# One product for the last 64 tokens of seven batches, and loads that wait for the transposed q

## The chip, the cores and the metric

The kernel runs on one core of a Trainium2 chip. The metric is the device time of one execution in microseconds (us). The kernel before takes 296.39 us, the median of three runs from 295.75 to 305.15.

## The reference

Inputs are q, k and v of shape (batch 8, heads 8, 576 tokens, 64 features) and two weight matrices. The first half is a linear attention whose feature map is a ReLU weighted by the cosine and the sine of the token's position; the second half is a feed-forward network with a sigmoid-approximated gelu.

```python
q_p = phi(q, cos_w, sin_w)          # max(x,0)*cos, max(x,0)*sin: 128 features
k_p = phi(k, cos_w, sin_w)
kv = einsum('bhsf,bhsd->bhfd', k_p, v);  z = sum(k_p over s)
num = einsum('bhsf,bhfd->bhsd', q_p, kv)
den = einsum('bhsf,bhf->bhs', q_p, z) + 1e-6
x = (num / den) as (8*576 tokens, 512)
h = x @ w_in                        # 512 -> 2048
out = (h * sigmoid(1.702*h)) @ w_out   # 2048 -> 512
```

## The kernel before

The work goes batch by batch, and the kernel calls the work of one batch a block. Instructions run on each engine in the order in which the program lists them; the order is written out by hand, and only the waits between engines are added by the framework.

A block b has two stages on TensorE. In the first, `mm1` multiplies w_in by the transposed x of the batch: for each of 16 groups of 128 hidden features (fc) four matmuls of 512 columns, that is 512 of the 576 tokens, followed by a gelu on ScalarE. The other 64 tokens of the batch, its tail, go through `mm1_tail`, where each of 64 matmuls loads a 128x128 block of w_in and streams 64 columns (L284). In the second stage `mm2` multiplies by w_out, 16 matmuls of 512 columns for each group of 128 tokens. Groups t = 0 to 3 are the 512 tokens of the batch. Group t = 4 is made of two tails, that of an even batch and that of the odd one after it; it is computed in the odd blocks, ahead of t = 0. Each group is copied out of PSUM by ScalarE (L309) to one of four ysb buffers and stored by a DMA on POOL's queue (L312).

Beside the matmuls of block b, the attention of batch b+1 is prepared. Early in the block VectorE computes the features of q (`trig_q`, L154), and SyncE issues five DMA transposes that write qT (`qturn_dma`, L184), the fifth with the 64 tail tokens. Once q's buffer has been read, POOL issues the load of q for batch b+2 (`load_q`, L112 and L114); then VectorE computes the features of k (L141) and copies v (L162), and POOL issues the loads of k and v (`load`, L109). With fc = 15 TensorE computes kv (L202). During the second stage it computes the numerator and denominator of five token groups (`num_mm`, L215), VectorE divides (`num_div`, L223 to L227), and SyncE issues a DMA transpose of each result into the x of the next block (`xturn_dma`, L253), four pieces of 128 tokens and one of 64. Numbers 0 to 3 come between halves of t = 0 and t = 1, number 4 in t = 2.

POOL's queue is one list: loads and stores are issued in the order of the program, and a store that is not ready holds the loads after it. DMAs issued by POOL run on queue q0, those issued by SyncE, the transposes among them, on q1; both use the same 16 DMA engines.

Blocks 0 and 1 differ: batch 0 is loaded in a different layout, the pipeline is filled, the weights are loaded in between, and block 1's first five feature groups are computed in four pieces of columns. In block 0 POOL already waits once for the transposed q (L415) before it loads the inputs of batch 2.

Of the kernel before, what the change touches and what calls it, by code (L numbers as in the profile page):

```python
# [9 lines left out]
F32 = mybir.dt.float32  # L10
BF16 = mybir.dt.bfloat16
AF = mybir.ActivationFunctionType
# [7 lines left out]
def kernel(  # L20
# [9 lines left out]
    nc = tc.nc  # L30
    B, H, S, D = q.shape
    d_model = H * D
    d_ff = moe_w_in.shape[1]
    KC = d_model // 128
    FC = d_ff // 128
    NS = S // 64
    MT = 512
# [3 lines left out]
    one = ctx.enter_context(tc.tile_pool(name="one", bufs=1))  # L41
    xpool = ctx.enter_context(tc.tile_pool(name="xpool", bufs=2))
    gpool = ctx.enter_context(tc.tile_pool(name="gpool", bufs=20))
    ypool = ctx.enter_context(tc.tile_pool(name="ypool", bufs=4))
    small = ctx.enter_context(tc.tile_pool(name="small", bufs=3))
    pmm = ctx.enter_context(tc.tile_pool(name="pmm", bufs=4, space=PSUM))
# [51 lines left out]
    qT = one.tile([128, H, 640], BF16, name="qT")  # L98
    w_in_sb = one.tile([128, KC, d_ff], BF16, name="w_in_sb")
    w_out_sb = one.tile([128, FC, d_model], BF16, name="w_out_sb")  # L100
# [7 lines left out]
    def load(t, src, b):  # L108
        nc.gpsimd.dma_start(out=t, in_=src_of(src, b))  # L109

    def load_q(b):
        nc.gpsimd.dma_start(out=qf[:, 0:2048].rearrange("p (h e) -> p h e", h=H),  # L112
                            in_=q[b, :, 0:512, :].rearrange("h (p c) d -> p h (c d)", c=4))
        nc.gpsimd.dma_start(out=qf[0:64, 2048:2560].rearrange("p (h e) -> p h e", h=H),  # L114
                            in_=q[b, :, 512:S, :].rearrange("h p d -> p h d"))
# [7 lines left out]
    gate = const.tile([1, 4], F32)  # L123
# [10 lines left out]
    def trig(dst, src, j, act=False):  # L134
        i = src[:, :, ts(j, 64)]
        for cs, w in enumerate((cosw, sinw)):
            o = dst[:, j, :, ts(cs, 64)]
            if act:
                nc.scalar.activation(o, i, AF.Relu, scale=w[:, j:j + 1])
            else:  # L140
                nc.vector.tensor_scalar(o, i, 0.0, w[:, j:j + 1], op0=MAX, op1=MUL)  # L141

    def trig_q(c, act=False):
        n = 128 if c < 4 else 64
        if c < 4:
            i = qf[:, 0:2048].rearrange("p (h c d) -> p c h d", h=H, c=4)[:, c]
        else:
            i = qf[0:64, 2048:2560].rearrange("p (h d) -> p h d", h=H)
        for cs, w in enumerate((cosw, sinw)):
            o, sc = qn[0:n, c, :, ts(cs, 64)], w[0:n, NS + c:NS + c + 1]  # L150
            if act:
                nc.scalar.activation(o, i, AF.Relu, scale=sc)
            else:
                nc.vector.tensor_scalar(o, i, 0.0, sc, op0=MAX, op1=MUL)  # L154

    def vcopy(i0, i1, act=False):
        o = vt[:, :, i0:i1, 0:64].rearrange("p j i e -> p i j e")
        i = vf[:, i0:i1].rearrange("p i (j e) -> p i j e", e=64)
        if act:
            nc.scalar.activation(o, i, AF.Copy)  # L160
        else:
            nc.vector.tensor_copy(o, i)  # L162
# [19 lines left out]
    def qturn_dma(c):  # L182
        n = 128 if c < 4 else 64
        nc.sync.dma_start_transpose(out=qT[:, :, c * 128:c * 128 + n],  # L184
                                    in_=qn[0:n, c].rearrange("p h f -> p (h f)"))
# [3 lines left out]
    def kv_open(i0=0, i1=NI):  # L189
        t = pat.tile([128, 2, 512], F32, name="at")  # L190
        for i in range(i0, i1):
            st["kv", i] = t[:, :, ds((i - i0) * 65, 65)]
        st["ps", i0] = t[:, :, 0:(i1 - i0) * 65]
        if i0 == 0:
            st["kvs"] = small.tile([128, 2, NI, VW], BF16, name="kvs", bufs=2)
# [9 lines left out]
    def kv_evac(i0, i1):  # L205
        o = st["kvs"][:, :, i0:i1, 0:65]
        nc.vector.tensor_copy(o, st["ps", i0].rearrange("p hh (i e) -> p hh i e", e=65))  # L207
# [23 lines left out]
    x = {}  # L231

    def x_open(b):
        x[b] = xpool.tile([128, KC, S], BF16, name="xT")

    def xturn_mm(c):
        ps, xn = nums[c]
# [5 lines left out]
    def xturn_evac(b, c):  # L243
        ps = nums.pop(c)[0]
        n = 128 if c < 4 else 64
        i = ps[:, :, 264:392].bitcast(BF16).rearrange("p a (k t) -> p a k t", k=2)[:, :, :, 0:n]
        o = x[b][:, :, c * 128:c * 128 + n].rearrange("p (a k) t -> p a k t", a=2)
        nc.scalar.activation(o, i, AF.Copy)

    def xturn_dma(b, c):  # L250
        xn = nums.pop(c)[1]
        n = 128 if c < 4 else 64
        nc.sync.dma_start_transpose(out=x[b][:, :, c * 128:c * 128 + n],  # L253
                                    in_=xn[0:n].rearrange("p a h e -> p (a h e)"))


    gT = {}
# [14 lines left out]
    def mm1(b, fc):  # L272
        mm1_part(b, fc, 0, MT)
        gelu(fc)

    gt = {}

    def mm1_tail(b, half):
        if half == 0 and b % 2 == 0:
            gt[0] = gpool.tile([128, FC, 128], BF16, name="gtail", bufs=2)  # L280
        hps = pmm.tile([128, 8, 64], F32, name="mm")
        for f in range(8):
            for kc in range(KC):
                nc.tensor.matmul(hps[:, f], w_in_sb[:, kc, ts(half * 8 + f, 128)], x[b][:, kc, MT:S],  # L284
                                 start=(kc == 0), stop=(kc == KC - 1))
        nc.scalar.activation(gt[0][:, ts(half, 8), ts(b % 2, 64)], hps, AF.Gelu_apprx_sigmoid)  # L286

    yp = {}
    out_j = out[0:S].rearrange("(p j) d -> j p d", j=NS)

    def rows(b, t):

        if t == 4:
            return [(64 * u, 64, out_j[NS - 1] if b + u == 1 else out[(b + u) * S - 64:(b + u) * S])
                    for u in range(2)]
        if b == 0:
            return [(64 * u, 64, out_j[2 * t + u]) for u in range(2)]
        return [(0, 128, out[b * S:b * S + 512].rearrange("(p c) d -> c p d", c=4)[t])]

    def mm2(b, t, lo, hi, c0=0, c1=d_model, last=False):  # L300
        if lo == 0:
            yp[t, c0] = pmm.tile([128, d_model], F32, name="mm")
        for fc in range(lo, hi):
            w = gT[fc][:, ts(t, 128)] if t < 4 else gt[0][:, fc, :]
            nc.tensor.matmul(yp[t, c0][:, c0:c1], w, w_out_sb[:, fc, c0:c1],  # L305
                             start=(fc == 0), stop=(fc == FC - 1))
        if hi == FC:
            ysb = ypool.tile([128, d_model], F32, name="ysb")
            nc.scalar.activation(ysb[:, c0:c1], yp[t, c0][:, c0:c1], AF.Identity)  # L309
            for p0, n, dst in rows(b, t):  # L310
                eng = nc.sync if last else nc.gpsimd
                eng.dma_start(out=dst[:, c0:c1], in_=ysb[p0:p0 + n, c0:c1])  # L312
# [78 lines left out]
    qturn_pe(4)  # L391
    qevac(4)
    x_open(0)
    start_block(0)

# [9 lines left out]
        trig(kr, kf, j)  # L405
    for fc in range(5, FC):
        mm1(0, fc)
    mm1_tail(0, 0)
    mm1_tail(0, 1)
    for c in range(5):  # L410
        trig_q(c, act=(c > 2))
        qturn_dma(c)
# [34 lines left out]
    for b in range(1, B):  # L447
        nb = b + 1 if b + 1 < B else None
        f0 = 5 if b == 1 else 0
        for fc in range(f0, FC):  # L450
            if nb is not None and fc == f0:
                for c in range(5):
                    trig_q(c)
                    qturn_dma(c)
                if nb + 1 < B:
                    load_q(nb + 1)
            if nb is not None and fc == f0 + 1:
                for j in range(NS):
                    trig(kr, kf, j)
                vcopy(0, 4)  # L460
                if nb + 1 < B:
                    load(kf, k, nb + 1)
                    load(vf, v, nb + 1)
            if nb is not None and fc == 15:
                kv_open()
                kv_mm(0, 4, vt_rhs, 0, 65)
                kv_evac(0, 4)
            mm1(b, fc)
        mm1_tail(b, 0)
        mm1_tail(b, 1)  # L470
        if nb is not None:
            x_open(nb)
        if b % 2:
            mm2(b, 4, 0, FC)
        for t in range(4):
            last = nb is None and t == 3
            if last:
                mm2(b, t, 0, FC, 0, 256)
                mm2(b, t, 0, FC, 256, 512, last=True)
                continue  # L480
            mm2(b, t, 0, 8)
            if nb is not None and t < 3:
                num_mm(2 * t)
                num_div(2 * t)
                xturn_dma(nb, 2 * t)
            mm2(b, t, 8, 16)
            if nb is not None and t < 2:
                num_mm(2 * t + 1)
                num_div(2 * t + 1)
                xturn_dma(nb, 2 * t + 1)  # L490
# [30 lines left out]
```

## Time and profile before

| | us |
|---|---|
| median of the runs | 296.39 |
| profiled execution, its own time | 295.57 |
| its span, first to last instruction | 293.9 |
| TensorE busy (share of the span) | 283.1 (96%) |
| first product, 512 columns and pieces (L264) | 113.6 |
| second product of the 512 tokens (L305) | 116.0 |
| first product of the tails (L284) | 16.2 |
| second product of the tails (L305 from gtail) | 13.6 |
| numerator (L215) and kv (L202, from vt) | 15.9 and 8.8 |
| VectorE busy, ScalarE busy | 123.8, 128.0 |
| DMA queue q0 / q1, share of 16 engines | 43.3% / 28.4% |

Busy time counts an instruction from its start to its modelled end, and overlapping matmuls are counted once. Below, a chain in order of time lists what TensorE did without such overlap: start, duration, engine and line, and how many instructions were merged. Of a DMA the profile gives the issue on the queue of the engine that starts it, and the time from issue to landing.

In block 1 the first product starts at 52.3 us, kv runs at 66.95, the tail at 69.11, t = 4 at 71.03, the first numerator at 76.15 and the next block at 89.45. Block 2 lasts from 89.45 to 121.45, block 3 from there to 156.91.

### The profile page before, as it was taken

Reading aid. Unit: us, or ns where it says so; the run is one execution under the profiler, and the core shown is the slowest. Engines: PE = TensorE matmul, PEld = TensorE weight load, DVE = VectorE, ACT = ScalarE, POOL = GpSimd, SP = SyncE. Lnnn points to the kernel's source line nnn. Section 1 sums busy time; section 2 is a strip of 40 time slices with the busy share of each in tenths; the row PEclk is TensorE's granted clock in tenths of the full one; section 3 lists DMA queues with packets and bytes.
Section 4 is the critical chain, followed back from the end, with each engine's and each line's share of the span. In section 5 each row is a group of like instructions: output and inputs, shape, how many; then the busy total and the mean of one; then the engine's idle time right before and its main releaser. Section 6 shows DMA issues by size and latency. Waiting matters only on the chain.

```text
span 293.9 us, 6796 instructions
## 1 busy us (share of the span) xinstructions
PE 283.1 (96%) x2832; PEld 155.7 (53%) x2871; DVE 123.8 (42%) x355; ACT 128.0 (44%) x220; POOL 81.9 (28%) x96
## 2 busy tenths in 40 slices
PE   8879999999999999999999999999999999999993
PEld 4775546746544465446454465446454465445443
DVE  4674513791369125930269115950159304200000
ACT  7847642674115721465114641265114651166121
POOL 6361002635216501470215601290114300100111
PEclk9999999999999999999999999999999999999999
DMA  7999997999999876779249983889258402400112
GB/s 254 239 219 276 351 180 109 326 312 228 323 272 184 240 294 142 156 192 365 71 128 171 221 333 96 151 193 386 85 140 153 93 2 75 115 36 0 38 71 73
DMA packets 64238, 53.59 MB, mean 182 GB/s; under 512 B 49552, under 2 KB 56336, under 8 KB 64208
## 3 DMA queue, kind: packets, MB, share of 16 engines
q0 software_dynamic: 13792, 38.87, 43.3%
q1 hardware_dynamic: 50416, 14.30, 28.4%
q8 instruction: 22, 0.36, 0.5%
q14 instruction: 8, 0.07, 0.1%
HBM read 36.70 MB, written 9.44 MB: 157 GB/s over the span
## 4 chain that ended last, share of the span: by engine, by line
PE 95%; issue 1%; DVE 1%; ACT 1%; ACTq 0%
PE mm L305 42%; PE mm L264 37%; PE mm L284 5%; PE at L202 4%; PE at L215 3%; PE mm L317 3%; PE at L241 1%; DVE xn L227 1%; PE mm L170 1%; ACT g L269 1%; DVE inv L225 0%; DVE den L223 0%; ACT ysb L309 0%; DVE warm L76 0%; ACTq L269 0%
## 5 line engine op out<-in xcount | busy, mean ns | idle before, releaser
L305 PE MATMUL mm<-w_out_sb,g 128*128 128x512 bf16 (+1 forms) x509 | 116.0, 372 | 1.1 <-issue 0.2
L264 PE MATMUL mm<-xT,w_in_sb 128*128 128x512 bf16 (+1 forms) x593 | 113.6, 345 | 0.8
L312 POOL DMA_DIRECT2D out_dram<-ysb x44 | 50.7, 1152 | 169.7 <-ACT ysb L309 162.9
L269 ACT ACTIVATE g<-mm 128x512 bf16<-128x512 f32 x128 | 75.6, 598 | 39.6 <-PE mm L264 39.6
L264 PEld LDWEIGHTS <-w_in_sb 128*128 128x128 bf16 x608 | 53.8, 98 | 55.2
L305 PEld LDWEIGHTS <-g 128*128 128x128 bf16 x528 | 49.0, 98 | 50.2
L309 ACT ACTIVATE ysb<-mm 128x512 f32<-128x512 f32 (+1 forms) x37 | 21.7, 586 | 108.1 <-PE mm L305 101.9
L223 DVE TENSOR_SCALAR den<-at 128x8 f32<-128x8 f32 x40 | 6.6, 166 | 60.6 <-PE at L215 60.6
L227 DVE TENSOR_TENSOR xn<-at,inv 128x512 bf16<-128x512 f32 x40 | 27.7, 691 | 2.4 <-DMA xT<-xn 1.0
L207 DVE CAST kvs<-at 128x520 bf16<-128x520 f32 (+1 forms) x9 | 5.8, 642 | 51.3 <-PE at L202 51.2
L141 DVE TENSOR_SCALAR kr<-kf,cosw 128x256 bf16<-128x256 f32 x68 | 23.8, 350 | 6.9 <-DMA kf<-in_k_dram 6.9
L141 DVE TENSOR_SCALAR kr<-kf,sinw 128x256 bf16<-128x256 f32 x68 | 23.1, 340 | 0.0
L215 PEld LDWEIGHTS <-qT 128*128 128x128 bf16 x320 | 14.5, 97 | 7.3
L154 DVE TENSOR_SCALAR qn<-qf,cosw 128x512 bf16<-128x512 f32 (+1 forms) x33 | 15.8, 478 | 3.9 <-DMA qf<-in_q_dram 3.9
L284 PEld LDWEIGHTS <-w_in_sb 128*128 128x128 bf16 x512 | 16.0, 98 | 1.9
L284 PE MATMUL mm<-xT,w_in_sb 128*128 128x64 bf16 x512 | 16.2, 193 | 0.1
L215 PE MATMUL at<-kvs,qT 128*128 128x65 bf16 x320 | 15.9, 193 | 0.0
L154 DVE TENSOR_SCALAR qn<-qf,sinw 128x512 bf16<-128x512 f32 (+1 forms) x33 | 15.8, 479 | 0.0
L305 PE MATMUL mm<-w_out_sb,gtail 128*128 128x512 bf16 x60 | 13.6, 379 | 0.2
L202 PEld LDWEIGHTS <-kr 64*128 64x128 bf16 x648 | 10.1, 94 | 4.3 <-issue 3.7
L286 ACT ACTIVATE gtail<-mm 128x512 bf16<-128x512 f32 x16 | 9.6, 597 | 5.1 <-PE mm L284 5.1
L317 PE MATMUL mm<-warm 128*128 128x64 bf16 (+1 forms) x114 | 8.7, 240 | 1.3 <-DVE warm L76 1.3
(54 smaller groups left out, 112.0 us busy)
## 6 DMA issues: line engine op xcount, KB each, us to landing
kf<-in_k_dram POOLq DMA_DIRECT2D x7, 1152.0 KB, 9.1
vf<-in_v_dram POOLq DMA_DIRECT2D x7, 1152.0 KB, 11.8
qf<-in_q_dram POOLq DMA_DIRECT2D x7, 1024.0 KB, 7.4
out_dram<-ysb POOLq DMA_DIRECT2D x27, 256.0 KB, 2.8
out_dram<-ysb POOLq DMA_DIRECT2D x17, 128.0 KB, 7.2
w_in_sb<-in_moe_w_in_dram POOLq DMA_DIRECT2D x4, 512.0 KB, 9.7
w_out_sb<-in_moe_w_out_dram POOLq DMA_DIRECT2D x4, 512.0 KB, 18.0
qf<-in_q_dram POOLq DMA_DIRECT2D x7, 128.0 KB, 7.4
```

Of the source, the lines that this page charges most:

```text
L141: nc.vector.tensor_scalar(o, i, 0.0, w[:, j:j + 1], op0=MAX, op1=MUL)
L154: nc.vector.tensor_scalar(o, i, 0.0, sc, op0=MAX, op1=MUL)
L202: nc.tensor.matmul(st["kv", i][:, hh, ds(col, n)], kr[r, j, i, :], rhs(r, i, j), start=(j == 0), stop=(j == NS - 1))
L215: nc.tensor.matmul(ps[:, h // 4, ds((h % 4) * 65, 65)], qT[:, h, ts(c, 128)], st["kvs"][:, hh, i, 0:65], start=True, stop=True)
L227: nc.vector.tensor_tensor(xn, pv[:, :, :, 0:64], inv.unsqueeze(3).to_broadcast([128, 2, 4, 64]), op=MUL)
L264: nc.tensor.matmul(hp[fc][:, t0:t1], w_in_sb[:, kc, ts(fc, 128)], x[b][:, kc, t0:t1], start=(kc == 0), stop=(kc == KC - 1))
L269: nc.scalar.activation(g, hp.pop(fc), AF.Gelu_apprx_sigmoid)
L284: nc.tensor.matmul(hps[:, f], w_in_sb[:, kc, ts(half * 8 + f, 128)], x[b][:, kc, MT:S], start=(kc == 0), stop=(kc == KC - 1))
L305: nc.tensor.matmul(yp[t, c0][:, c0:c1], w, w_out_sb[:, fc, c0:c1], start=(fc == 0), stop=(fc == FC - 1))
L309: nc.scalar.activation(ysb[:, c0:c1], yp[t, c0][:, c0:c1], AF.Identity)
L312: eng.dma_start(out=dst[:, c0:c1], in_=ysb[p0:p0 + n, c0:c1])
L317: nc.tensor.matmul(w[:, 0:cols], warm[:, 0:128], warm[:, 0:cols], start=True, stop=True)
```

## The change

The transposed tails of all batches go to one tile, xt, of 8 x 64 columns, and their gelus to one tile, gt, likewise. The tail of batch 0 is computed in block 0 as before. Those of batches 1 to 7 are computed in the last block: for each of the 16 feature groups four matmuls of 448 columns and one gelu. The second product of all four pairs of tails follows there, ahead of t = 0; blocks 1, 3 and 5 have no t = 4 any more. In blocks 1 to 5, a copy of one element of qT on POOL stands ahead of the load of q, so that the loads of q, k and v, and what is queued on POOL behind them, wait until the last transpose of q has landed.

```diff
     def x_open(b):
-        x[b] = xpool.tile([128, KC, S], BF16, name="xT")
+        x[b] = xpool.tile([128, KC, MT], BF16, name="xT")
+
+    def x_cols(b, c):
+        return x[b][:, :, ts(c, 128)] if c < 4 else xt[:, :, ts(b, 64)]
...
-    def mm1_tail(b, half):
-        if half == 0 and b % 2 == 0:
-            gt[0] = gpool.tile([128, FC, 128], BF16, name="gtail", bufs=2)
+    xt = one.tile([128, KC, B * 64], BF16, name="xt")
+    gt = one.tile([128, FC, B * 64], BF16, name="gt")
+
+    def mm1_tail_first(half):
         hps = pmm.tile([128, 8, 64], F32, name="mm")
         for f in range(8):
             for kc in range(KC):
-                nc.tensor.matmul(hps[:, f], w_in_sb[:, kc, ts(half * 8 + f, 128)], x[b][:, kc, MT:S],
+                nc.tensor.matmul(hps[:, f], w_in_sb[:, kc, ts(half * 8 + f, 128)], xt[:, kc, 0:64],
                                  start=(kc == 0), stop=(kc == KC - 1))
...
+    def mm1_tails(fc):
+        hps = pmm.tile([128, MT], F32, name="mm")
+        for kc in range(KC):
+            nc.tensor.matmul(hps[:, 64:B * 64], w_in_sb[:, kc, ts(fc, 128)], xt[:, kc, 64:B * 64],
+                             start=(kc == 0), stop=(kc == KC - 1))
+        nc.scalar.activation(gt[:, fc, 64:B * 64], hps[:, 64:B * 64], AF.Gelu_apprx_sigmoid)
...
-            w = gT[fc][:, ts(t, 128)] if t < 4 else gt[0][:, fc, :]
+            w = gT[fc][:, ts(t, 128)] if t < 4 else gt[:, fc, ts(b // 2, 128)]
...
                 if nb + 1 < B:
+                    nc.gpsimd.tensor_copy(gate[0:1, 3:4], qT[0:1, 7, S - 1:S])
                     load_q(nb + 1)
...
             mm1(b, fc)
-        mm1_tail(b, 0)
-        mm1_tail(b, 1)
         if nb is not None:
             x_open(nb)
-        if b % 2:
-            mm2(b, 4, 0, FC)
+        else:
+            for fc in range(FC):
+                mm1_tails(fc)
+            for u in range(1, B, 2):
+                mm2(u, 4, 0, FC)
```

More of the change, by code (lines that the diff above doesn't have):

```diff
@@ L246, in xturn_evac @@
         i = ps[:, :, 264:392].bitcast(BF16).rearrange("p a (k t) -> p a k t", k=2)[:, :, :, 0:n]
-        o = x[b][:, :, c * 128:c * 128 + n].rearrange("p (a k) t -> p a k t", a=2)
+        o = x_cols(b, c).rearrange("p (a k) t -> p a k t", a=2)
         nc.scalar.activation(o, i, AF.Copy)
@@ L252, in xturn_dma @@
         n = 128 if c < 4 else 64
-        nc.sync.dma_start_transpose(out=x[b][:, :, c * 128:c * 128 + n],
+        nc.sync.dma_start_transpose(out=x_cols(b, c),
                                     in_=xn[0:n].rearrange("p a h e -> p (a h e)"))
@@ L274, in mm1 @@
         gelu(fc)
-    gt = {}
-    def mm1_tail(b, half):
-        if half == 0 and b % 2 == 0:
-            gt[0] = gpool.tile([128, FC, 128], BF16, name="gtail", bufs=2)
+    xt = one.tile([128, KC, B * 64], BF16, name="xt")
+    gt = one.tile([128, FC, B * 64], BF16, name="gt")
+    def mm1_tail_first(half):
         hps = pmm.tile([128, 8, 64], F32, name="mm")
@@ L283, in mm1_tail @@
             for kc in range(KC):
-                nc.tensor.matmul(hps[:, f], w_in_sb[:, kc, ts(half * 8 + f, 128)], x[b][:, kc, MT:S],
+                nc.tensor.matmul(hps[:, f], w_in_sb[:, kc, ts(half * 8 + f, 128)], xt[:, kc, 0:64],
                                  start=(kc == 0), stop=(kc == KC - 1))
-        nc.scalar.activation(gt[0][:, ts(half, 8), ts(b % 2, 64)], hps, AF.Gelu_apprx_sigmoid)
+        nc.scalar.activation(gt[:, ts(half, 8), 0:64], hps, AF.Gelu_apprx_sigmoid)
+    def mm1_tails(fc):
[4 more added lines that the diff above has]
+        nc.scalar.activation(gt[:, fc, 64:B * 64], hps[:, 64:B * 64], AF.Gelu_apprx_sigmoid)
     yp = {}
@@ L301, in mm2 @@
         if lo == 0:
-            yp[t, c0] = pmm.tile([128, d_model], F32, name="mm")
+            yp[b, t, c0] = pmm.tile([128, d_model], F32, name="mm")
         for fc in range(lo, hi):
-            w = gT[fc][:, ts(t, 128)] if t < 4 else gt[0][:, fc, :]
-            nc.tensor.matmul(yp[t, c0][:, c0:c1], w, w_out_sb[:, fc, c0:c1],
+            w = gT[fc][:, ts(t, 128)] if t < 4 else gt[:, fc, ts(b // 2, 128)]
+            nc.tensor.matmul(yp[b, t, c0][:, c0:c1], w, w_out_sb[:, fc, c0:c1],
                              start=(fc == 0), stop=(fc == FC - 1))
@@ L308, in mm2 @@
             ysb = ypool.tile([128, d_model], F32, name="ysb")
-            nc.scalar.activation(ysb[:, c0:c1], yp[t, c0][:, c0:c1], AF.Identity)
+            nc.scalar.activation(ysb[:, c0:c1], yp[b, t, c0][:, c0:c1], AF.Identity)
             for p0, n, dst in rows(b, t):
@@ L407 @@
         mm1(0, fc)
-    mm1_tail(0, 0)
-    mm1_tail(0, 1)
+    mm1_tail_first(0)
+    mm1_tail_first(1)
     for c in range(5):
```

## The prediction

> **What bounds the kernel now.** I read the shares of busy time, then the chain that ended last, then the waits, then the DMA views of the one place where something is close.
>
> ```profile
> PE 283.1 (96%) x2832; PEld 155.7 (53%) x2871; DVE 123.8 (42%) x355; ACT 128.0 (44%) x220; POOL 81.9 (28%) x96
> PE 95%; issue 1%; DVE 1%; ACT 1%; ACTq 0%
> L284 PEld LDWEIGHTS <-w_in_sb 128*128 128x128 bf16 x512 | 16.0, 98 | 1.9
> L284 PE MATMUL mm<-xT,w_in_sb 128*128 128x64 bf16 x512 | 16.2, 193 | 0.1
> ```
>
> TensorE is the bound: the chain is 95% TensorE, and among the waits after 50 us TensorE has none at all. So a microsecond of matmul taken out is a microsecond gained, as long as nothing else becomes late; and any wait of TensorE that the change makes is lost in full, since there is no idle time to absorb it. L284, the 64-column product of the tail, keeps the weight loader busy as long as the array (16.0 against 16.2 us).
>
> **The tail product.** The chain in order of time gives each piece without the overlap of the pipeline.
>
> ```profile
> 53.87 0.89 PE mm L264 x16
> ...
> 104.56 1.87 PE mm L284 x64
> 106.43 0.22 PE mm L305
> 106.70 1.46 PE mm L305 x6
> 108.16 0.24 PE at L215 x8
> 108.40 1.73 PE mm L305 x8
> ```
>
> A tail of one batch is 64 matmuls in 1.87 us, 29.2 ns each. Seven go: 13.1 us. In their place come 64 matmuls of 448 columns, a width the trace does not show. The nearest rows bound it: 128 columns take 0.89/16 = 55.6 ns, 512 take 1.73/8 = 216 ns, so 64 cost between 3.6 and 13.8 us; the line between the two gives 189 ns at 448, and I take 64 x 189 = 12.1 us. The gain is 13.1 - 12.1 = **1.0 us** (never below -0.7, by the 512 row). It is small because a 64-column matmul already ran at 29 ns.
>
> The gelu after it: fourteen of 0.6 us (L286) become sixteen of some 0.55 us (between the 0.38 us of the 256-column copy and the 0.60 us of 512). One comes every 4 x 189 = 756 ns of TensorE, so ScalarE keeps up and this costs nothing; without cover it would be 0.2 us per gelu. The second product of the tails moves from blocks 1, 3, 5 into block 7: four times 3.45 us are still four times 3.45 us. Their stores go to the POOL queue one every 3.45 us, with 2.8 us to landing, so the four ysb buffers hold; the last token group and its store stay where they were.
>
> **What becomes late.** Block 1 loses both its tail (1.87) and its second tail product (3.45): everything after its first product comes 5.3 us earlier, at first without its loads being any earlier. Blocks 3 and 5 lose the same, blocks 2, 4, 6 lose 1.87. So I look at the transfers of block 1 (SyncE's transposes, POOL's loads).
>
> ```profile
> L184 SPq DMA_TRANSPOSE qT<-qn x1: 2042/2042/2042, 69.0 to 69.0; - x1
> DMA to landing us min/median/max: 13.8/13.8/13.8
> ```
> ```profile
> 66.88 0.92 POOL L112 DMA_DIRECT2D qf<-in_q_dram  x1
> ...
> 69.25 0.75 POOL L109 DMA_DIRECT2D vf<-in_v_dram  x1
> ...
> 77.59 10.04 SPq L253 DMA_TRANSPOSE xT<-xn  x5
> ...
> 83.87 0.41 PE L215 MATMUL at<-kvs,qT 128*128 128x65 bf16 x8
> ```
>
> The first fence is the last transpose of q for batch 2: issued at 69.0, landed at 82.8, used by TensorE at 83.87. That use moves to 78.6. Without the new hold it would cause a stall of about 4 us there. With it the loads (q, k, v of batch 3) wait, and the transposes have the engines alone.
>
> ```profile
> q0 software_dynamic: 95, 0.37, 100.6%
> q1 hardware_dynamic: 95, 0.02, 10.7%
> ...
> q1 hardware_dynamic: 839, 0.21, 118.2%
> ```
>
> These are two slices of one microsecond: in 79 to 80, beside the loads (q0), the transposes' queue moved 95 packets; in 90 to 91, alone, 839. From 72 to 84 it moved 887, 74 per us. A transposed piece of x is 128 KB in 256-byte packets, 512 of them.
>
> Step by step for block 1 after the change (times of the trace of before, TensorE's shifted by -5.3):
> 1. The last piece of q's transpose: its issue ended at 71.04. In block 2 that piece landed 1.5 us after its issue ended (94.1 + 2.7 against 95.3). I take a landing at **72.3**, 71.3 to 73.5 as bounds. It is in time for 78.6.
> 2. The hold: in block 0 the same gate saw its landing at 49.2 and the load was issued at 49.96, so the load goes at 72.3 + 0.76 = 73.0 instead of 66.88. Behind the gate on POOL wait both q loads, k, v and then the stores of block 1, of which the first is ready at about 73.4; no ysb buffer runs out, as there are four for four stores.
> 3. The loads' bulk: at 96.49 the issue was followed by data from 98.0 to 108.5 (10.5 us, 332 GB/s). So here 74.5 to 85.0, and two stores of 0.26 MB that stand behind them in the same queue add 1.4: it ends at 86.4. The same stretch with transposes beside it took 12.5 us in before (71.5 to 84), its two stores included.
> 4. The transposes of x for batch 2 are issued at 72.3, 74.3, 76.2, 78.2 (77.6, 79.6, 81.5, 83.5 less 5.3). The first is through before the data of the loads comes (2.4 us in block 2). The other three, 1,536 packets, move 74 per us beside the loads: 75.0 to 86.4 is some 840. The remaining 700 take 0.9 us alone, and the last lands at about 87.7.
> 5. The first product of block 2 reads all four pieces (mm1_part takes columns 0 to 512 of x), and it would start at 89.45 - 5.3 = 84.1. **TensorE waits 3.6 us.** Bounds: nothing, if pieces land 2.7 us after issue as in block 2 (80.9); 6.9 us, if the bulk ends at 87.2 and the last piece follows by 3.8 us, as 87.7 followed 83.9 in before, which makes 91.0.
>
> In before the same piece landed at 87.7 for a start at 89.45, a margin of 1.75 us, with the loads issued 10.7 us ahead of the first x transpose. Now they are issued at the same time.
>
> **The later blocks.** There the hold costs about 1 us: in block 2 POOL was free to load at 96.49 only because its store's issue had taken 6.07 us, and the last piece of q lands at 96.8. Loads at block start + 8.2 are through at + 20; x transposes, issued from + 18.4 to + 24.3, land by + 27, and the block is now 30.1 us long. Three us of margin: cost nothing; if it were gone, it would show five times. The gate copy itself (0.17 us on POOL) is on no path.
>
> Sum, against the profiled execution's own 295.57 us (span 293.9, 1.7 us around it): 295.57 - 1.0 + 3.6 = **298.2 us**, +0.9%. The median of the runs, 296.39, is 0.8 us above the profiled one, which shifts nothing in the reasoning. Two per cent is about what a measurement of this kernel can tell from no change; the forecast lies within it.
>
> **The clock.** A rule speaks against a wait of this length. First the row, at the end of this trace:
>
> ```profile
> 289.00:290.00 1.00, 0.36 (x4) 0.08 (x1) 0.00 (x0) 0.38 (x1) 0.00 (x0) 1.00 0.37 131
> ...
> 292.00:293.00 1.00, 0.00 (x0) 0.00 (x0) 0.00 (x0) 0.00 (x0) 0.00 (x0) 0.84 0.00 0
> 293.00:293.90 0.90, 0.00 (x0) 0.00 (x0) 0.00 (x0) 0.00 (x0) 0.00 (x0) 0.50 0.00 0
> ```
>
> The columns end in granted clock, DMA share and GB/s; TensorE stops at 289.4, the clock falls to 0.50 at 292.7 (0.84 in that slice), 3.3 us later. The price of a slow clock, from the start of the trace: the first twelve 512-column matmuls filled 1.3 to 6.1 us, 4.8 us for what takes 12 x 0.216 = 2.6 later, so 2.2 us lost (the clock column does not show that stretch as slow). The Trainium skill, "TensorE: Matmul & The Clock Gate", Part 1, says that the clock is halved after an idle window of about 3.4 us whose phase runs free, so that a gap must cover one whole window. By it a wait of 3.6 us would seldom trip and the sum stays 298.2; tripping would cost half a window, 1.7 us, and give 299.9, an estimate from that page.
>
> **The rivals.**
> A. No wait (20%): the transposes of x get through beside the loads, or the loads' bulk is short. For it: in block 2 pieces land in 2.3 to 3.5 us. Against it: no load was running there. 295.57 - 1.0 = 294.6, up to 296.5 with a wait under 2 us.
> B. Slower by over 2% (14%): the wait before block 2 is 4.5 to 6.9 us, long enough for the clock to fall, 2.2 us more. 295.57 - 1.0 + 4.5 + 2.2 = 301.3 to 303.7. It decides when x's last piece lands after about 88.6. For it: q's pieces issued at 57.6 and 59.1 into the middle of a load landed 9.1 and 9.5 us later.
> C. The hold is late in every block (3%): the margin of 3 us is used up and five boundaries wait 1 us or more, 303 and above. Against it: q's transposes were over by block start + 7.4.
> D. The hold does nothing in block 1, because q's last piece lands at 82 whatever the loads do (2%): the wait goes to the numerator at 78.6 and the loads start at 83; 301 to 306. Against it: the slow landing coincides with the loads' packets.
> The forecast (2 to 4.5 us of wait, 296.6 to 299.1, to 300 with a clock drop) has 60%; faster by over 2% would need 5.9 us, which no row offers: 1%.
>
> The range takes in A and most of B: 294.4 to 302.6. Within 2%: A, the forecast and a part of B, 83%; slower 16%; faster 1%.
>
> **What the profile after would show.** The 64-column group with 64 instead of 512; 64 matmuls of 448 columns in about 12.1 us in block 7; no wait of TensorE for the transposed q near 78; a wait of 3.6 us for x's DMA between blocks 1 and 2 at 84 and at no other boundary; load of batch 3 issued near 73. I am wrong if that wait is absent, if it recurs, or if 448 columns take over 200 ns.

## The result and the profile after

The changed kernel takes 309.37 us, the median of six runs from 306.51 to 310.5; the kernel before 296.1 us. The ratio is 1.0441, 95% interval 1.0386 to 1.0497: slower by 4.4%. Medians are of all executions, but the ratios here and below leave out slow ones, those more than 1.5% above the fastest of the same kernel (when the changed kernel was measured again, two of four). The forecast was 298.2 us, with a range to 302.6. The profiled execution is the shortest of the six, 306.51 us with a span of 304.8 us, so the trace accounts for 10.9 us more than the span of before, 293.9; what the longer runs add to that is in no trace.

The page's shares of busy time, its chain, and the groups of the tails' first product (the tail of batch 0 is left at L287):

```profile
PE 285.9 (94%) x2487; PEld 149.1 (49%) x2487; DVE 124.2 (41%) x355; ACT 128.3 (42%) x222; POOL 76.7 (25%) x101
PE 86%; DMA 8%; DVE 3%; issue 1%; ACT 0%; ACTq 0%
...
L294 PE MATMUL mm<-xt,w_in_sb 128*128 128x448 bf16 x64 | 12.3, 352 | 0.0
```

TensorE was 95% of the chain and is 86%; DMA has come in with 8%. Part of that stands in the first 70 us, where the chain now runs through the load of k and VectorE without TensorE having lost time: kv starts at 66.83, at 66.95 before. What TensorE lost is in the view of its waits after 20 us: who waited, for whom, us in total, how often, and the longest.

```profile
PE mm L267 <- DMA xT<-xn: 9.9, 1, 9.9
PE at L202 <- DVE vt L162: 0.3, 1, 0.3
```

One wait of 9.9 us, for the DMA transposes of x. The chain in order of time shows where (start, duration, engine and line, instructions merged):

```profile
76.94 1.19 PE mm L315 x6
78.13 15.81 DMA xT<-xn
93.94 0.09 issue
94.03 14.79 PE mm L267 x60
...
120.83 5.18 PE mm L315 x24
126.01 12.95 PE mm L267 x60
...
260.37 12.11 PE mm L294 x64
```

It is the start of block 2, for the fourth piece of x, issued at 78.13 and landed at 93.94. The 60 matmuls after it take 14.79 us, where the same 60 of block 3 take 12.95: 1.84 us more. The clock says why (the last three columns are granted clock, DMA share and GB/s, the first pair is the stretch and its length):

```profile
86.00:87.00 1.00, 0.00 (x0) 0.00 (x0) 0.04 (x1) 0.00 (x0) 0.00 (x0) 1.00 1.00 391
87.00:88.00 1.00, 0.00 (x0) 0.00 (x0) 1.00 (x4) 0.00 (x0) 0.00 (x0) 0.61 1.01 393
...
94.00:97.00 3.00, 2.97 (x8) 1.05 (x9) 0.00 (x0) 0.60 (x1) 0.00 (x0) 0.50 1.15 237
97.00:98.00 1.00, 1.00 (x5) 0.45 (x4) 0.00 (x0) 0.37 (x1) 0.00 (x0) 0.77 1.00 184
```

TensorE stops at 84.1, where block 2 would have begun. By the shares in the slices that hold the changes, the clock halves at about 87.2 and is whole again at about 97.5, 3.5 us after the matmuls have begun again. The last line of the chain is the wide product: 64 matmuls of 448 columns in 12.11 us. The sum is -13.1 + 12.1 + 9.9 + 1.84 = +10.7 us of the 10.9 by which the span grew.

POOL's queue in block 1, and the landing of x's fourth piece:

```profile
73.06 0.17 POOL L466 CAST gate<-qT 1x1 f32<-1x1 bf16 x1 [6.17 <-DMA qT<-qn]
73.60 0.93 POOL L112 DMA_DIRECT2D qf<-in_q_dram  x1 [0.37 <-DVE inv L225]
...
85.06 0.54 POOL L322 DMA_DIRECT2D out_dram<-ysb  x1 [2.80 <-ACT ysb L319]
```
```profile
L256 SPq DMA_TRANSPOSE xT<-xn x1: 1605/1605/1605, 78.1 to 78.1; - x1
...
DMA to landing us min/median/max: 15.8/15.8/15.8
```

The hold does what it says: POOL waits 6.17 us for the transposed q, and the loads go at 73.6 instead of 66.9. Four stores follow them, the last at 85.06. The piece of x lands 15.8 us after its issue.

### The profile page after: what moved, and what is told of

Read it like the earlier page. It is cut to its first block, busy times and chain, and to the rows that moved or that the text cites. A ratio compares the mean times of both kernels' runs of the same rounds, so it can differ in the third digit from the quotient of the medians.

```text
span 304.8 us, 6119 instructions
## 1 busy us (share of the span) xinstructions
PE 285.9 (94%) x2487; PEld 149.1 (49%) x2487; DVE 124.2 (41%) x355; ACT 128.3 (42%) x222; POOL 76.7 (25%) x101
## 4 chain that ended last, share of the span: by engine, by line
PE 86%; DMA 8%; DVE 3%; issue 1%; ACT 0%; ACTq 0%
PE mm L315 39%; PE mm L267 33%; DMA xT<-xn 5%; PE mm L294 4%; PE at L202 4%; DMA kf<-in_k_dram 3%; PE at L215 3%; PE mm L327 3%; DVE kr L141 2%; DVE xn L227 1%; PE mm L170 1%; PE mm L287 1%; PE at L244 1%; DVE vt L162 0%; DVE inv L225 0%
## 5 line engine op out<-in xcount | busy, mean ns | idle before, releaser
L267 PE MATMUL mm<-xT,w_in_sb 128*128 128x512 bf16 (+1 forms) x608 | 116.2, 349 | 10.0 <-DMA xT<-xn 9.9
L315 PE MATMUL mm<-w_out_sb,g 128*128 128x512 bf16 (+1 forms) x528 | 117.4, 372 | 0.0
L267 PEld LDWEIGHTS <-w_in_sb 128*128 128x128 bf16 x608 | 54.1, 98 | 66.7 <-issue 12.6
L322 POOL DMA_DIRECT2D out_dram<-ysb x44 | 44.5, 1012 | 160.5 <-ACT ysb L319 153.1
L154 DVE TENSOR_SCALAR qn<-qf,cosw 128x512 bf16<-128x512 f32 (+1 forms) x33 | 15.8, 479 | 4.5 <-DMA qf<-in_q_dram 4.5
L154 DVE TENSOR_SCALAR qn<-qf,sinw 128x512 bf16<-128x512 f32 (+1 forms) x33 | 15.8, 479 | 0.0
L315 PE MATMUL mm<-w_out_sb,gt 128*128 128x512 bf16 x64 | 14.0, 379 | 0.0
L294 PE MATMUL mm<-xt,w_in_sb 128*128 128x448 bf16 x64 | 12.3, 352 | 0.0
L296 ACT ACTIVATE gt<-mm 128x448 bf16<-128x448 f32 x16 | 8.7, 544 | 3.3 <-PE mm L294 3.2
L315 PEld LDWEIGHTS <-gt 128*128 128x128 bf16 x64 | 6.2, 97 | 7.5
```

What stands on the lines that cost most here:

```text
L267: nc.tensor.matmul(hp[fc][:, t0:t1], w_in_sb[:, kc, ts(fc, 128)], x[b][:, kc, t0:t1], start=(kc == 0), stop=(kc == KC - 1))
L294: nc.tensor.matmul(hps[:, 64:B * 64], w_in_sb[:, kc, ts(fc, 128)], xt[:, kc, 64:B * 64], start=(kc == 0), stop=(kc == KC - 1))
L315: nc.tensor.matmul(yp[b, t, c0][:, c0:c1], w, w_out_sb[:, fc, c0:c1], start=(fc == 0), stop=(fc == FC - 1))
```

## The experiments

The question is why one wait of 3.6 us became one of 9.9 and more. Theory: x's transposes of batch 2 pass beside the loads of batch 3, which the hold has moved on top of them, and land when these are through. Rivals: the shorter block is the whole cost and the hold none of it; or the transposes are slow in this place whatever is loaded.

**One part of the change at a time.** First the change without the hold (e1).

```diff
                 if nb + 1 < B:
-                    nc.gpsimd.tensor_copy(gate[0:1, 3:4], qT[0:1, 7, S - 1:S])
                     load_q(nb + 1)
```

> The change without the hold: POOL loads batch 3 as early as before (about 66.9 us). Theory, that x's transposes of batch 2 are slowed packet by packet beside the loads: the last piece of q lands at about 82.8 as in before, its numerator, due at 78.6, waits about 4 us; x's pieces land near 87.7 and the next block starts at 88.3, so no second wait. With 1.0 us gained by the wide matmuls: about 299 us, 300.5 if the clock falls. Rival, that the 5.3 us by which block 1 is shorter are the whole cost and the hold adds nothing: the same 10 us wait for x as in the changed kernel, 307 us or more.

302.17 us, ratio 1.0209 (1.0180 to 1.0238). The line of the waits, and the chain behind it:

```profile
PE at L215 <- DMA qT<-qn: 4.8, 1, 4.8
```
```profile
69.53 14.74 DMA qT<-qn
84.28 0.04 issue
84.32 0.62 PE at L215 x8
84.94 6.00 PE mm L315 x18
```

The wait is the expected one, at the expected place: the last piece of q takes 14.7 us to land beside the loads. There is no second wait. The 18 matmuls after it take 6.00 us, 333 ns each instead of 216: the clock fell here too. The time is 1.7 us above the upper expectation.

Then the kernel before with the hold alone (e2), the same line added in front of its load of q.

> The kernel before with the hold alone, tails as they were. Theory: the loads of batch 3 go at about 73.5, as in the changed kernel, x's pieces are issued at 77.6 to 83.5 beside them and the last one lands at about 94, where block 2 would start at 89.45: a wait of 4.5 us, and if the clock falls 2 us more, 300 to 302.5 us. Rival, that the hold is harmless and the missing 5.3 us of block 1 are all: 296 us, no wait of TensorE for x.

299.71 us, ratio 1.0128 (1.0093 to 1.0164).

```profile
PE mm L264 <- DMA xT<-xn: 2.5, 1, 2.5
PE at L202 <- DVE vt L162: 0.7, 1, 0.7
```

The hold by itself makes TensorE wait for x, in a block of full length. The load went at 73.34, x's fourth piece was issued at 85.7 and landed at 92.5. In the changed kernel, with the load at 73.6, the same piece was issued 7.6 us earlier, at 78.1, and landed no earlier, at 93.9: the landing goes with the loads and not with the issue. So neither rival "the hold is harmless" nor "the hold is all" holds: each part is slower alone, by 2.1% and 1.3%, with intervals clear of 1. Together they cost the sum or more: the hold saves the wait for q, but the shorter block takes 5.3 us of margin from the wait for x that the hold makes.

**Keep block 1 as long as it was.** Batches 0 and 1 keep their tails, six are gathered, and there is no hold (e3).

```diff
-            nc.tensor.matmul(hps[:, 64:B * 64], w_in_sb[:, kc, ts(fc, 128)], xt[:, kc, 64:B * 64],
+            nc.tensor.matmul(hps[:, 128:B * 64], w_in_sb[:, kc, ts(fc, 128)], xt[:, kc, 128:B * 64],
...
                 if nb + 1 < B:
-                    nc.gpsimd.tensor_copy(gate[0:1, 3:4], qT[0:1, 7, S - 1:S])
                     load_q(nb + 1)
...
+        if b == 1:
+            mm1_tail_first(1, 0)
+            mm1_tail_first(1, 1)
...
-            for u in range(1, B, 2):
+            for u in range(3, B, 2):
                 mm2(u, 4, 0, FC)
+        if b == 1:
+            mm2(1, 4, 0, FC)
```

> No hold; batches 0 and 1 keep their own tails and block 1 its second tail product, the tails of batches 2 to 7 are gathered in the last block with 384 columns. Theory: block 1 is as long as in before and nothing waits; gained are six times 1.87 us, spent 64 matmuls of 384 columns, by the line of 55.6 and 216 ns 163 ns each, 10.4 us: 0.8 us net, about 295.3 us and a ratio near 0.997. Rival, that the later blocks have become too short for their transfers without the hold: waits at the start of blocks 3 to 7, over 297 us.

295.62 us, ratio 0.9996 (0.9971 to 1.0022), and TensorE waits for no DMA after 20 us. The expected 0.997 lies at the edge of the interval; a gain is not shown. What is shown is that the later blocks need no hold and bear their shorter length.

**Move the loads away from x.** In block 1 the loads of batch 3 wait for the transposed x instead of the transposed q (e4).

```diff
-                if nb + 1 < B:
+                if nb + 1 < B and b > 1:
                     nc.gpsimd.tensor_copy(gate[0:1, 3:4], qT[0:1, 7, S - 1:S])
                     load_q(nb + 1)
...
-                if nb + 1 < B:
+                if nb + 1 < B and b > 1:
                     load(kf, k, nb + 1)
                     load(vf, v, nb + 1)
...
                 xturn_dma(nb, 2 * t + 1)
+                if b == 1 and t == 1:
+                    nc.gpsimd.tensor_copy(gate[0:1, 3:4], x[nb][0:1, KC - 1, MT - 1:MT])
+                    load_q(nb + 1)
+                    load(kf, k, nb + 1)
+                    load(vf, v, nb + 1)
```

> The change, but in block 1 the loads of batch 3 are held until the transposed x of batch 2 has landed (piece 3), not q. Theory: x's pieces, alone, land 2.4 to 3 us after their issue, the last at about 81, block 2 starts at 84.1 without a wait; the loads go at about 81.5 and v lands at 95.5, VectorE is done with it at about 99 and kv, due at 97, waits about 2 us: about 297 us. Rival, that x's transposes are slow by themselves in this place (the engines stood still there from 80 to 83): the wait at 84 stays above 5 us and the time above 301.

306.37 us, ratio 1.0343 (1.0311 to 1.0375).

```profile
PE mm L267 <- DMA xT<-xn: 7.9, 1, 7.9
PE at L202 <- DVE vt L162: 2.7, 2, 1.6
```
```profile
104.07 1.23 PE mm L315 x6
105.30 19.56 DMA xT<-xn x2
124.86 0.14 issue
124.99 5.02 PE mm L267 x13
```

Both the expectation and its rival missed. Block 2 starts without a wait for x: its pieces were issued from 73.5 to 81.4 and landed 2.4 to 3.7 us later, so they are not slow there by themselves. But the time was not won. The loads of batch 3 went at 82.9, so q's transposes for batch 3 landed only at 103.9, the hold of block 2 let the loads of batch 4 go at 104.6, and these met the transposes of x for batch 3. The collision had moved on by one block, and the wait of 7.9 us stands at the start of block 3. I had not followed the delay past its own block.

**How much is mixed.** Next the volume beside x's transposes in block 1: without the load of v (e5), and with the four stores put off to block 2 (e6).

```diff
                     load(kf, k, nb + 1)
-                    load(vf, v, nb + 1)
+                    if b > 1:
+                        load(vf, v, nb + 1)
```

> The changed kernel, but in block 1 the load of v for batch 3 is left out (v of batch 2 is used again, so batch 3's part of the output is not the reference's). Theory, that x's last piece lands when the loads' bulk is over: the bulk is 1.18 MB shorter, at 0.27 to 0.37 MB per us 3.2 to 4.4 us, so TensorE waits 5.5 to 6.7 us instead of 9.9 and the time falls by 3 to 5 us, to about 305 against 309.4 (profiled 306.5). Rival, that the transposes of this place are slow by themselves or stand still from 80 to 83 whatever is loaded: the wait stays at 9 to 10 us and the time within 1 us.

305.39 us, ratio 1.0309 (1.0280 to 1.0337). The time is 4.0 us below the 309.37 of the changed kernel, as the theory has it; but the wait in its profile, from an execution of 306.1 us, is hardly shorter:

```profile
PE mm L267 <- DMA xT<-xn: 9.5, 1, 9.5
```

```diff
+            if b == 1 and t < 4:
+                late[t] = one.tile([128, d_model], F32, name=f"late{t}")
+                nc.scalar.activation(late[t], yp[b, t, c0], AF.Identity)
+                return
...
+            if b == 2 and fc == 8:
+                for t in range(4):
+                    for p0, n, dst in rows(1, t):
+                        nc.gpsimd.dma_start(out=dst, in_=late[t][p0:p0 + n])
             mm1(b, fc)
```

> The changed kernel, but the four stores of block 1 go to buffers of their own and are issued in block 2 after its eighth feature group, so that they don't stand behind the loads of batch 3. Theory: 1.05 MB less before x's last piece, 2.8 to 3.9 us, so the wait is 6 to 7 us and the time 2.5 to 4 us shorter than that of the changed kernel. Rival, that the stores pass after the transposes are through anyway and only the loads count: wait and time as before this edit.

305.14 us, ratio 1.0278 (1.0230 to 1.0326), 4.2 us less than 309.37, with a wait of 8.2 us. In both runs the time is lower by about what was expected and the wait of the one profile by less than that. But the changed kernel measured again, below, has a ratio of 1.0345 (1.0301 to 1.0389), which overlaps with both, so it is not shown that either edit made the kernel faster. A mean rate for the volume does not describe what happens. The DMA of the stretch from 79 to 84 us (queue, packets, MB, share of 16 engines) is of before, of the changed kernel, and of the one with later stores in turn:

```profile
q0 software_dynamic: 457, 1.76, 94.0%
q1 hardware_dynamic: 567, 0.14, 12.9%
```
```profile
q0 software_dynamic: 214, 0.83, 91.5%
q1 hardware_dynamic: 420, 0.10, 10.1%
```
```profile
q0 software_dynamic: 120, 0.52, 98.7%
q1 hardware_dynamic: 272, 0.07, 9.5%
```

The time that q0's packets took is over 90% of the 16 engines' in all three, yet q0 moves 0.83 MB and 0.52 MB where before it moved 1.76. So in these 5 us both queues are slow, and a packet takes longer: 16 engines times 5 us, times the share, over the packets makes 0.16, 0.34 and 0.66 us for one of q0. From 84 us on the changed kernel's loads are fast again. Its microsecond from 89 to 90:

```profile
q0 software_dynamic: 107, 0.37, 91.4%
q1 hardware_dynamic: 106, 0.02, 10.5%
```

The two queues pass nearly packet for packet, as 95 and 95 did in the prediction's slice of before: one 256-byte packet of a transpose for one of some 3.5 KB on q0. In such a stretch x gets on no faster than the loads do.

**X without DMA.** In block 1 the five pieces of x are transposed by TensorE and copied out by ScalarE, as in block 0 (e7).

```diff
+                if b == 1 and t > 0:
+                    xturn_mm(2 * t - 1)
+                    xturn_evac(nb, 2 * t - 1)
                 num_mm(2 * t)
                 num_div(2 * t)
-                xturn_dma(nb, 2 * t)
+                if b > 1:
+                    xturn_dma(nb, 2 * t)
             mm2(b, t, 8, 16)
+            if nb is not None and t < 3 and b == 1:
+                xturn_mm(2 * t)
+                xturn_evac(nb, 2 * t)
...
-                xturn_dma(nb, 2 * t + 1)
+                if b > 1:
+                    xturn_dma(nb, 2 * t + 1)
```

> The changed kernel, but in block 1 the five pieces of x for batch 2 are transposed by TensorE and copied out by ScalarE, as block 0 does, and not by DMA. Theory, that x's DMA transposes beside the loads are the only thing that is late: no wait of TensorE at block 2's start, and no clock drop; five times 0.22 us of TensorE are added and 1.0 us is gained, span about 294 and time 295.7, ratio 1.00. Rival, that the loads of batch 3 themselves (issued at 73.6 instead of 66.9) are late for block 2: the wait comes back at the kv product or at the features of q, and the time stays over 299.

296.74 us, ratio 1.0027 (1.0005 to 1.0049).

```profile
PE mm L267 <- DMA xT<-xn: 0.9, 1, 0.9
PE at L202 <- DVE vt L162: 0.7, 1, 0.7
```

The wait before block 2 is gone, with the loads where the hold put them; the 0.9 us stand at the start of block 3. So the loads' delay as such makes block 2 wait for nothing, and what is late is x's way through the DMA engines. The 0.7 us is a wait for v in block 1, ahead of all that this edit changes: kv starts at 66.95 in the trace of before and between 66.6 and 68.1 in those of these runs.

**The changed kernel again (e8), and two smaller loads (e9, e10).**

> The changed kernel itself once more, beside the next two: a second profile of it. Theory, that x's pieces wait for whatever is mixed with them on the DMA engines, volume by volume: the time is again 306 to 310 us with one wait of 10 to 13 us for x ahead of block 2, and slices between 75 and 92 us in which both queues move little. Rival, that the profile of the changed kernel was an accident of one execution: another place or another size.

308.26 us, median of four from 305.45 to 310.82, ratio 1.0345 (1.0301 to 1.0389). The profile, of the execution of 305.45 us, has the wait at the same place, below the 10 to 13 us that were expected: TensorE stops at 84.1 and goes on at 92.9, 8.8 us, x's fourth piece landing at 92.8.

With only q of batch 3 loaded in block 1:

```diff
                     load_q(nb + 1)
...
-                if nb + 1 < B:
+                if nb + 1 < B and b > 1:
                     load(kf, k, nb + 1)
                     load(vf, v, nb + 1)
```

> The changed kernel, but block 1 loads only q of batch 3, not k and v (those of batch 2 are used again, so batch 3's part of the output is not the reference's): 1.15 MB of loads instead of 3.5. Theory, that the wait goes by the volume that is mixed with x's transposes: q's data is through at about 79 and the two first stores at 81, x's last piece lands at 81 to 84, TensorE waits 0 to 1 us, about 296 us. Rival, that mixing by itself makes the engines stand still for several us, whatever the volume (without v, the wait was still 9.5 us): a wait of 4 us or more and over 300 us.

299.54 us, ratio 1.0128 (1.0098 to 1.0158), between the two expectations.

```profile
PE mm L267 <- DMA xT<-xn: 2.9, 1, 2.9
```
```profile
87.00:88.00 1.00, 0.55 (x3) 0.25 (x4) 1.00 (x5) 0.00 (x0) 1.00 (x1) 0.89 1.14 331
88.00:89.00 1.00, 1.00 (x4) 0.43 (x3) 1.00 (x6) 0.00 (x0) 1.00 (x1) 0.50 1.37 163
```

X's fourth piece landed at 87.4, 3.4 us or more later than the theory gives for so small a load. The clock fell all the same, at about 87.8, after a gap of 2.9 us.

And with no load of batch 3 in block 1, `load_q` skipped there as well:

> The changed kernel without any load of batch 3 in block 1 (batch 2's inputs are used again, so batch 3's part of the output is not the reference's); only the four stores are left beside x's transposes. Both theories: no wait, x's pieces land 2.4 to 4 us after issue, the clock does not fall, about 295 us. If there is a wait all the same, the transposes are late in this place without any load.

294.61 us, ratio 0.9979 (0.9947 to 1.0011), no wait of TensorE for x; its pieces land 2.4 to 4.3 us after issue.

Put in order by what is loaded beside x's transposes, the waits of the profiles are 0 (nothing), 2.9 (q, 1.18 MB), 9.5 (q and k, 2.4 MB) and 9.9 and 8.8 us (all, 3.5 MB); the medians are 294.6, 299.5, 305.4 and 308 to 309 us, where the step from the third to the last is not shown to be more than the scatter. The loads beside x are shown to be the cause: without them the wait is gone (e10), and without x's DMA as well (e7). The wait does not grow evenly with the volume, and why both queues slow down together between about 79 and 84 us is not settled. It is in the profiles of the changed kernel (0.83 and 1.22 MB on q0 from 79 to 84), without v (0.63) and with the stores later (0.52); neither of these two edits took it away.

One part of it coincides with something else in the traces. A microsecond in which few packets pass follows a packet of q8, the queue that the profile calls instruction: in before q8's packet starts between 75 and 76 and 36 packets of q0 pass from 77 to 78; in the changed kernel between 80 and 81, and 16 pass from 82 to 83; with q alone between 82 and 83, and 2 pass from 83 to 84. That one causes the other is not shown, and it is not the whole: with the stores later 7 packets of q0 pass from 80 to 81, ahead of q8's.

## Why the prediction was wrong

*Place and mechanism.* These were right, and not by luck, as the runs without the loads and without x's DMA show. One wait, of x for batch 2, at 84.1, at no other boundary, with the last piece of q in time; blocks 3 to 6 are 30.1 us long and wait for nothing, so rival C was rightly small. Rival D did not occur: q's last piece landed at 73.0 with the loads held. None of the three signs of being wrong came; there was none for a longer wait.

*The wide product.* 12.11 us for 64 matmuls of 448 columns, 189 ns each, as the line between the two rows gave. By the rows, 13.1 less 12.1, the gain of 1.0 us is there; in a whole time no run shows it clear of zero (0.9979, 0.9947 to 1.0011, without the loads).

*The term that was mis-sized* is step 4, the landing of x's fourth piece, and with it step 3, the end of the loads; so the wait of step 5 came to 9.9 us instead of 3.6. Forecast against measured:

| | forecast | measured |
|---|---|---|
| last piece of q lands | 72.3 | 73.0 |
| load of q is issued | 73.0 | 73.6 |
| loads' data begins | 74.5 | 75 |
| q0's bulk ends | 86.4 | about 91.5 |
| x's fourth piece: issued, landed | 78.2, 87.7 | 78.1, 93.9 |
| TensorE waits | 3.6 | 9.9 |

Of the 6.2 us by which the landing was late, 0.5 is the start. I counted two stores behind the loads, but four were issued before the bulk was through (at 76.7, 77.7, 81.6 and 85.1): q0 moved 4.56 MB from 75 to 92, not 4.0, some 1.4 us more at 0.37 MB per us. From 79 to 84 it moved 0.93 MB less than the same stretch before, 2.5 us at that rate. And from the end of the bulk to the landing 2.4 us passed instead of 1.3. That leaves 0.7 us that I can't place. The step's own sum was also off: 86.4 and 0.9 make 87.3, and no reason is given for the 0.4 us up to 87.7.

*What was wrong in the reasoning.* I priced the transposes with the mean rate of the mixture in before (74 packets per us), and the loads with that of a load in block 2 (332 GB/s), near the 0.33 MB per us of that mixture. The mixture had a slow patch of its own (0.17 MB on q0 from 77 to 78), but it was short, and I took the mean as the rate of a steady process. My upper bound of 6.9 us was no bound: it moved the bulk's end by only 0.8 us and let the landing be late by 3.8. Bounds for a transfer that competes should have come from the worst landing under load in the trace, the 13.8 us of q's last piece, which was shown in the prediction itself. Added to the issue at 78.2 it gives 92.0, and a wait of 7.9 us, still 2 us short of the measured one.

*The clock.* Rival B had the right mechanism at 14%; its wait was still too short. Its price, 2.2 us against 1.84, was near partly by luck, as it came from a stretch in which the clock column shows no fall; in the five profiles in which the clock falls ahead of block 2 or in it (the changed kernel, e5, e6, e8, e9), the first 60 matmuls of the block took 14.79 to 15.80 us, 1.84 to 2.85 more than 12.95. I used the rule of the Trainium skill, "TensorE: Matmul & The Clock Gate", Part 1, to call a fall after 3.6 us seldom. Read as "a gap must cover a whole window of about 3.4 us", that did not hold: in e9 a gap of 2.9 us was enough, while in e2 one of 2.5 was not. But no length of the gap decides by itself. The falls come from 2.2 us (e8) to 5.2 us (e4) after the last matmul; in e9 matmuls had begun again shortly before. In e4 TensorE stops at 117.1, and the clock falls at 122.35:

```profile
122.00:123.00 1.00, 0.00 (x0) 0.00 (x0) 1.00 (x5) 0.00 (x0) 1.00 (x1) 0.68 1.12 215
```

Once down, it stayed so for 3.42 us (e9), 6.83 (e1) or 10.24 (the changed kernel): one, two and three times 3.41, as if it could change only in steps of that length. So the forecast's wait of 3.6 us could have gone either way: 298.2, or 300.0 with the fall.

## What to carry to other kernels

A hold that takes one transfer out of another's way puts its loads somewhere else; look at what they meet there, and one block further on, before counting it as free. Where the bound engine has no slack, a gain of 1 us by wider matmuls is worth less than the margin of the transfers that the shortened stage used up: check each transfer's landing against its use, as here 87.7 against 89.45. Price a transfer that shares the DMA engines at least by its worst landing under load, not by a mean rate.

## What the runs showed of the hardware

DMA transposes and large loads slow each other. At the loads' full rate they pass packet for packet, 106 and 107 in a microsecond of the changed kernel, where 839 packets of transposes passed alone (the prediction's slice of before); and from 79 to 84 us q0 moved 0.5 to 1.2 MB in four profiles, with its packets' time over 90% of the engines', where 1.76 MB passed in the mixture of before. A transpose of x that landed in 2.4 us alone took 15.8 beside the loads, in the same trace.

A gap of TensorE can cost more than itself: the clock halved 2.2 to 5.2 us after the last matmul, after a gap of 2.9 us (e9) but not after one of 2.5 (e2). It was whole again 3.4 us (the changed kernel) to 5.5 us (e6) after matmuls had begun again, which cost 1.84 us on top of the 9.9 in the changed kernel and 2.85 in e6.
